# Sink keys as rows of the window products, in units 2 to 7 of a fused attention and MoE kernel

## The chip, the core and the metric

The kernel runs on one core of one Trainium2 chip. Its time is the device time of that core in microseconds (us), the median of the timed runs. TensorE (PE) multiplies matrices: a stationary operand is loaded into the array (the profile lists these loads as PEld), and a moving operand streams past it, one column after the other. ScalarE (ACT), VectorE (DVE) and GpSimd (POOL) do the elementwise work; SyncE (SP) issues most transfers.

## What is computed

Attention over 4 batches of 8 heads, 768 positions, 64 numbers per head; then a two-layer network on the 3072 rows of 512. Heads 0, 2 and 6 are "retrieval" heads with a full causal mask. The other five are "streaming" heads: a query sees the first four keys (the sinks) and the last 64 keys up to itself.

```python
pos = np.arange(S); rel = pos[:, None] - pos[None, :]
causal = rel >= 0
is_sink = pos[None, :] < n_sink                    # 4
in_win = (rel >= 0) & (rel < window)               # 64
stream_keep = causal & (is_sink | in_win)
# retrieval heads: causal; the others: stream_keep
scores = np.where(mask, scale * q @ k.T, -1e9)
a = softmax(scores); attn = a @ v
x = attn.transpose(0, 2, 1, 3).reshape(B * S, H * D)
h = x @ w_in                                       # 512 -> 2048
out = (h * sigmoid(beta * h)) @ w_out              # 2048 -> 512
```

## The kernel before

The work is cut into eight **units** of 384 queries: unit n is batch n // 2 and half u = n % 2. Heads are worked in pairs, `PAIRS = [(0, 2), (1, 3), (4, 5), (6, 7)]`; one head of a pair lies in partitions 0 to 63, the other in 64 to 127. Scores are made transposed: keys on the 128 partitions, queries along the columns.

A planner inside the kernel (`_Plan`) puts all steps of all units in one order before anything is emitted. Each step has a key (`KEYS`, `WEIGHTS`), an engine, a rough cost, and what it needs; the instructions are then emitted in the planned order, and every engine works them off in that order. Where the planner leaves TensorE idle in unit 0's attention, it puts in **filler products** (`fill`), one for each 0.14 us of the gap, whose results are thrown away.

What a pair multiplies in one round (of unit half u), before:

```python
def rounds_of(pi, u):
    if u == 0:
        r = [[("r", 0, 0, 0, 384)], [("r", 1, 0, 128, 256), ("r", 2, 256, 256, 128)]]
    else:
        r = [[("r", j, 0, 0, 384)] for j in range(4)] + [[("r", 4, 0, 128, 256), ("r", 5, 256, 256, 128)]]
    s = []                                   # streaming: one product per 64 keys, up to 128 queries wide
    for c in range(CK * u - u, CK * (u + 1)):
        a = 0 if c == 1 else max(W * c - NQ * u, 0)
        z = min(W * (c + 2) - NQ * u, NQ)
        s.append(("s", c, a, a, z - a))
    kk = [("k", 0, 0, 0, NQ)]                # the sinks of all streaming heads
    if pi == 0: return [(a, a) for a in r]
    if pi == 3:                              # head 6 (retrieval) and head 7 (streaming)
        if u == 0: return [(r[0], s), (r[1], kk)]
        return [(r[0], s), (r[1], r[2]), (r[3], r[4]), (kk, None)]
    return [(s, s)]
```

`r` are retrieval products, `s` streaming ones (64 x 64 tiles of the array, so that four products can run side by side), and `k` the **sink product**: four products of 384 columns on 128 x 32 tiles of the array, with the sink keys in `KS`. Then come `exps` (ACT), `masks` (DVE), and on TensorE the sums of the exponentials and the product with v:

```python
def sums_d(x):                               # units 2 to 7
    for g, heads in enumerate(QUARTERS[x.u]):        # a column group of 32 for each quarter
        # ... one product per head and key block, with `one` as stationary operand
        if not all(RETR[h] for h in heads):
            ops.append((own_k[:, 4 if x.u else g, :], q1, NQ - q1, x.esk[0:96, q1:NQ]))   # the sinks

def pv(x, g):                                # two halves of heads, on 128 x 64 tiles, two side by side
    for t in (2 * g, 2 * g + 1):
        for i, h in enumerate(XT[t]):        # XT = [(1, 0), (2, 3), (4, 5), (6, 7)]
            if RETR[h]: ...                  # all key blocks: 768 columns in u = 0, 1920 in u = 1
            else:
                for m in range(CK):          # CK = 6 windows of 64 queries
                    if m * W == q0:          # q0 = 128 in u = 0, else 0
                        ops[i].append((NQ - q0, dst[:, q0:NQ], v_k[x.b][:, h, :], x.esk[0:96, q0:NQ], True, False))
                    # ... and one product of 64 columns with this window's two bands of v (vb or vs)
```

`v_k` holds the sinks' rows of v. It is made once in each batch by one product of 512 columns (`sink_rows`) and one multiplication on DVE. After `pv`, a unit's output is multiplied by the reciprocals of the sums, which go through DRAM to all partitions (`R`), into `xT`. Then the network: `mm1` (16 steps of four products of 384 columns), tanh on ACT, a multiplication on DVE, `mm2` (48 products of 512 columns), and the store. Steps of the network of earlier units stand between the attention steps of later units.

Of the kernel before, what the change touches and what calls it, by code (L numbers as in the profile page):

```python
# [20 lines left out]
NQ = 384  # L21
W = 64
# [7 lines left out]
ROWS = [16, 1]  # L30
ORDER = [[1, 0, 2, 3, 4, 5, 6, 7], [2, 6, 0, 3, 5, 7, 1, 4]]
# [3 lines left out]
    0: dict(lq=[-867.63, -728.31, -730.63, -861.49], lv=-338.14, C=[-364.52, -1117.07, -416.91, -454.59],  # L35
            T=[-593.39, -494.98, -308.07, -568.52], Q=[-267.24, -212.09, -319.35, -717.68],
            cv=[-309.34, -91.27, -785.19], vs=-175.72, vk=-519.21,
            B=[-492.15, -1098.07, -359.98, -568.46, -655.04, -421.48],
            E=[-761.34, -835.95, -537.15, -373.09, -160.62, -919.99],
            M=[-842.64, -436.28, -451.98, -264.53, -413.76, -592.08], S=-196.54, PV=[-406.98, -335.7], X=-688.47,  # L40
            F=[-47.22, -383.06, -14.57, -520.56], G=[-23.54, 44.75, 33.66, 67.09], H=-87.61, sb=-40.38,
            K=[-295.2, -917.7, -414.78]),
    1: dict(lq=[-424.63, -518.51, -317.21, -542.89], lv=-248.7, C=[-264.93, -110.02, -65.86, 1.78],
            T=[-592.79, -447.04, -134.08, -263.47], Q=[-86.97, -86.77, -472.24, -157.6],
            cv=[-104.39, -123.85, -204.22], vs=-111.06, vk=-227.51,
            B=[-728.8, -332.17, -375.19, -55.98, -37.26, -168.01, -724.86, -812.81, -32.31, -467.05, -96.54],
            E=[-299.76, -955.72, -117.13, -111.14, -506.53, -629.08, -272.67, -374.85, -407.81, -734.1, -557.24],
            M=[-448.13, 142.04, -287.39, -182.14, -214.76, -87.46, -561.74, -248.24, -363, -708.61, -250.48],
            S=-250.99, PV=[-538.57, -518.79], X=-72.99, F=[-62.61, -17.61, 44.38, -2.21],
            G=[58.84, 81.77, 74.93, 65.11], H=-332.45, sb=-201.63),  # L50
    2: dict(lq=[-416.41, -381.4, -375.23, -111.77], lv=-85.57, C=[-1.57, 131.34, 92.08, -0.63],
            T=[-7.79, -106.6, -279.89, -142.17], Q=[-127.57, 11.25, -176.77, -95.2], cv=[215.12, 152.27, -53.69],
            vs=532.03, vk=-98.63, B=[-100.36, -95.37, -260.42], E=[-56.84, -139.67, -194.81],
            M=[-251, -136.27, -105.29], S=-141.35, PV=[-99.98, -73.43], X=58.03, F=[-5.31, 68.88, 61.48, 105.62],
            G=[127.21, 90.09, 155.67, 145.53], R=7.33, K=[-41.03, 176.29, -207.29]),
    3: dict(lq=[-65.67], lv=352.93, C=[276.11, -311.81, -109.25], T=[-65.55, -186.26, 121.75],
            Q=[-27.36, 87.63, -69.21], cv=[303.29, 57.44, 13.83], vs=438.39, vk=191.75,
            B=[-126.86, -132.7, -389.02, -338.32, -42.23, 27.27],
            E=[-174.47, 110.62, -203.94, -257.91, 97.6, -63.29],
            M=[-216.92, -285.73, 28.13, -291.66, -162.48, 133.49], S=5.68, PV=[99.38, 46.54], X=77.71,  # L60
            F=[143.55, 87.99, 21.2, 161.21], G=[211.15, 159.59, 176.38, 124.95], R=-194.75),
    4: dict(lq=[213.64], lv=91.1, C=[-84.25, 214.91, 139.17], T=[-74.73, 137.47, -94.05],
            Q=[-116.26, -18.94, -19.03], cv=[37.21, 191.11, -24.92], vs=216.77, vk=-56.98, B=[63.19, -218.96, 56.7],
            E=[50.2, -22.44, -28.58], M=[-87.34, 62.45, 66.02], S=111.58, PV=[73.02, 72.41], X=-156.66,
            F=[178.96, 228.68, 227.28, 168.93], G=[228.49, 235.2, 212.64, 313.26], R=96.78,
            K=[-98.15, 333.15, -412.12]),
    5: dict(lq=[153.65], lv=283.14, C=[-371.96, 105.69, -99.7], T=[284.77, 136.35, 162.01], Q=[96.7, -6.95, 21.1],
            cv=[343.23, 362.82, 283.36], vs=280.24, vk=315.34, B=[-342.38, -103.18, 138.11, 126.61, -33.02, -1.01],
            E=[151.53, 220.73, 91.89, -241.66, -117.85, 178.48], M=[323.29, 126.63, -48.92, -97.8, -64.06, -284.52],
            S=189.85, PV=[-27.56, 59.94], X=-28.53, F=[246.54, 257.62, 228.44, 218.8],  # L70
            G=[370.19, 298.35, 241.7, 258.69], R=62.41),
    6: dict(lq=[145.75], lv=-48.06, C=[-100.29, 81.71, 55.44], T=[-6.35, -249.03, 190.12], Q=[33.29, 189.15, 130.92],
            cv=[22.17, -39.12, 3.11], vs=-109.11, vk=127.62, B=[-177.6, 246.99, 39.37], E=[252.37, 112.26, 238.38],
            M=[-25.1, 212.24, 357.65], S=68.68, PV=[-104.85, 76.59], X=-95.74, F=[375.04, 260.96, 368.28, 228.57],
            G=[388.65, 85.93, 323.69, 287.02], R=258.28, K=[14.01, -86.57, 0.8]),
    7: dict(lq=[111.55], lv=244.51, C=[-29.06, 38.68, 180.35], T=[-19.82, 321.37, -67.06],
            Q=[-170.86, -20.97, -73.78], cv=[76.79, 160.48, -152.51], vs=345.66, vk=-143.1,
            B=[289.56, 210.32, 223.69, -83.71, -272.2, 113.35], E=[-16, -92.33, -70.04, 333.97, -166.52, 23.53],
            M=[-57.51, -79.37, 15.22, 9.01, 57.77, -43.38], S=105.82, PV=[78.32, 140.51], X=-43.74,
            F=[420.59, 208.13, 325.41, -98.23], G=[328.32, 377.85, 148.63, 178], R=79.15),  # L80
}
WEIGHTS = dict(li=[-240.27, -225.8, -149.08, -105.34], lo=[-231.42, -185.85, -123.74, -8.12],
               ci=[-238.56, -234.45, -195.53, -74.09], co=[-115.86, -8.5, 18.95, 196.17], mask=[-672.86, -114.61],
               esel=-193.69, own=-44.44, sel=-79.94, sink=-196.29, table=-134.62, masks=-67.9, beta=-44.67)
GATES = [30, 47, 50, 64]
# [117 lines left out]
def kernel(  # L203
# [23 lines left out]
    def tpool(name, bufs, space=None):  # L227
# [4 lines left out]
        q2f=5, k2f=5, vf=3, wf=3, c=4, vb=2, vs=2, xT=2, gT=2, t=2, osb=3, R=1, sc=1, rec=1, hl=1, VK=2,  # L232
# [28 lines left out]
    identf = consts.tile([128, 128], F32, name="identf")  # L261
    mask_c = consts.tile([128, 128], BF16, name="mask_c")
    mask_s = [consts.tile([128, NQ], BF16, name=f"mask_s{u}") for u in range(2)]
    esel = consts.tile([128, 8, 4, 8], BF16, name="esel")
    esel_k = consts.tile([96, 4, 8], BF16, name="esel_k")
    beta_h = consts.tile([128, FO], F32, name="beta_h")
    odd = consts.tile([128, W], BF16, name="odd")
    even = consts.tile([128, W], BF16, name="even")
    sel = consts.tile([128, 8, D], BF16, name="sel")
    sel_c = consts.tile([128, 8], F32, name="sel_c")  # L270
    sel_k = consts.tile([128, 4, 2], F32, name="sel_k")
# [4 lines left out]
    own_k = consts.tile([96, 5, 32], BF16, name="own_k")  # L276
    warm = consts.tile([128, 1], F32, name="warm")
    QK = [consts.tile([128, 2, NP, S], BF16, name=f"QK{par}") for par in range(2)]
    KS = [[consts.tile([128, 32], BF16, name=f"KS{par}{pi}") for pi in range(1, NP)] for par in range(2)]
    sink_sel = consts.tile([128, 96], BF16, name="sink_sel")  # L280
    sink_own = consts.tile([96, H], F32, name="sink_own")
# [10 lines left out]
    def const_ident():  # L292
        pool.memset(warm, 0.0)
        pool.memset(identf, 1.0)
        aff(identf, 1, -1, 0, 128)
        aff(identf, -1, 1, 0, 128)
        dve.tensor_copy(out=ident, in_=identf)
# [4 lines left out]
    def const_masks():  # L302
        pool.memset(mask_c, 1.0)
        aff(mask_c, -1, 1, 0, 128)
        pool.memset(odd, 1.0)
        aff(odd, -1, 1, W, W)
        aff(odd, 1, -1, -1, W)
        pool.memset(even, 1.0)
        aff(even[0:W], -1, 1, 0, W)
        aff(even[W:2 * W], 1, -1, -1, W)  # L310
# [4 lines left out]
    def const_own():  # L315

        dve.memset(one, 0.0)
        dve.memset(one[:, 31:32], 1.0)
        dve.memset(own_k, 0.0)
        for u in range(2):  # L320
            for g, heads in enumerate(QUARTERS[u]):
                for i, h in enumerate(heads):
                    if not RETR[h]:
                        pi = [h in p for p in PAIRS].index(True)
                        dve.tensor_copy(out=own_k[:, 4 if u else g, ROWS[u] * i:ROWS[u] * i + 1],
                                        in_=sel_k[0:96, pi - 1, PAIRS[pi].index(h):PAIRS[pi].index(h) + 1])

    def const_zero():
        dve.memset(hl, 0.0)
        for par in range(2):  # L330
            for t in KS[par]:
                dve.memset(t, 0.0)

    def const_mask_s(u):
# [3 lines left out]
        if not u:  # L338
            dve.memset(mask_s[0][W:2 * W, 0:W], 0.0)
            dve.memset(mask_s[0][0:SINK, W:2 * W], 1.0)  # L340
# [98 lines left out]

    held = {}  # L440

    v_k = {}

    def sink_rows(b):

# [680 lines left out]
```

The softmax here doesn't subtract the row's maximum and nothing guards it: scores larger than these inputs give would overflow.

## Time and profile before

| | before |
|---|---|
| median time | 244.4 us |
| span of the profiled execution | 241.3 us |
| PE busy | 230.3 us (95%) |
| ACT busy | 146.4 us (61%) |
| DVE busy | 135.0 us (56%) |
| POOL busy | 79.1 us (33%) |
| transfers | 42.72 MB |

Busy time of PE is time in which at least one product is in the array; a product is counted with its way through the array, so that neighbours overlap. In the timeline the interval from one group's start to the next group's start is therefore the better measure of what a group costs. In the table of time stretches a number after a busy time, such as (x17), counts the instructions that touch the stretch. A tile shape such as 64*64 names the part of the array that a product uses.

### The profile page before, as it was taken

Reading aid. Unit: us, or ns where it says so; the run is one execution under the profiler, and the core shown is the slowest. Engines: PE = TensorE matmul, PEld = TensorE weight load, DVE = VectorE, ACT = ScalarE, POOL = GpSimd, SP = SyncE. Lnnn points to the kernel's source line nnn. Section 1 sums busy time; section 2 is a strip of 40 time slices with the busy share of each in tenths; the row PEclk is TensorE's granted clock in tenths of the full one; section 3 lists DMA queues with packets and bytes.
Section 4 is the critical chain, followed back from the end, with each engine's and each line's share of the span. In section 5 each row is a group of like instructions: output and inputs, shape, how many; then the busy total and the mean of one; then the engine's idle time right before and its main releaser. Section 6 shows DMA issues by size and latency. Waiting matters only on the chain.

```text
span 241.3 us, 5467 instructions
## 1 busy us (share of the span) xinstructions
PE 230.3 (95%) x2124; PEld 128.6 (53%) x2124; DVE 135.0 (56%) x313; ACT 146.4 (61%) x245; POOL 79.1 (33%) x170
## 2 busy tenths in 40 slices
PE   6879997999999999999999999999999999999994
PEld 6656663555444555446544545565465466546553
DVE  5678965788342477623764567576574058406610
ACT  2798762788536398661896278709864138408721
POOL 5233476686754466323745104230000000000000
PEclk9997999999999999999999999999999999999999
DMA  6999999999879997899999969993501620021012
GB/s 193 318 246 211 354 320 284 292 300 209 208 150 236 261 228 178 185 205 251 180 223 217 208 174 233 222 171 113 130 3 48 174 92 0 0 90 43 0 43 87
DMA packets 90570, 42.72 MB, mean 177 GB/s; under 512 B 74592, under 2 KB 83312, under 8 KB 90544
## 3 DMA queue, kind: packets, MB, share of 16 engines
q1 hardware_dynamic: 89424, 41.58, 76.7%
q10 hardware_dynamic: 1120, 0.79, 1.0%
q8 instruction: 16, 0.26, 0.5%
q14 instruction: 10, 0.08, 0.1%
HBM read 31.99 MB, written 6.37 MB: 159 GB/s over the span
## 4 chain that ended last, share of the span: by engine, by line
PE 84%; DMA 6%; ACT 3%; DVE 3%; POOL 2%; SPq 1%; issue 1%; POOLq 0%; ACTq 0%
PE b L103 73%; PE sp L103 11%; DMA wf<-in_moe_w_out_dram 3%; DMA wf<-in_moe_w_in_dram 3%; ACT es L103 2%; DVE QK L103 1%; POOL w_out L103 1%; ACT QK L103 1%; SPq L103 1%; DVE KS L103 0%; DVE b L103 0%; ACT c L103 0%; POOL identf L103 0%; POOL w_in L103 0%; DVE sel L103 0%
## 5 line engine op out<-in xcount | busy, mean ns | idle before, releaser
L103 DVE SCALAR_TENSOR_TENSOR gT<-t,b 128x384 bf16<-128x384 f32 x128 | 69.3, 551 | 51.9 <-ACT t L103 46.3
L103 PE MATMUL b<-xT,w_in 128*128 128x384 bf16 x512 | 89.7, 326 | 1.5 <-POOL w_in L103 1.5
L103 PE MATMUL b<-w_out,gT 128*128 128x512 bf16 (+1 forms) x400 | 90.5, 371 | 0.1
L103 ACT ACTIVATE t<-b,beta_h 128x384 f32<-128x384 f32 x128 | 72.9, 583 | 27.8 <-PE b L103 19.9
L103 PEld LDWEIGHTS <-w_in 128*128 128x128 bf16 x512 | 48.7, 98 | 38.7 <-issue 3.1
L103 PEld LDWEIGHTS <-gT 128*128 128x128 bf16 x400 | 37.3, 98 | 40.1 <-issue 2.9
L103 ACT ACTIVATE es<-sp 128x768 bf16<-128x768 f32 (+1 forms) x68 | 51.1, 799 | 11.9 <-PE sp L103 11.8
L103 ACT ACTIVATE osb<-b 128x512 f32<-128x512 f32 (+1 forms) x21 | 12.1, 578 | 35.4 <-PE b L103 35.3
L103 POOL CAST c<-wf 128x256 bf16<-128x256 f32 x60 | 23.2, 426 | 28.4 <-DMA wf<-in_q_dram 20.5
L103 PE MATMUL sp<-QK 64*64 64x128 bf16 (+5 forms) x420 | 19.6, 245 | 2.2 <-ACT es L103 0.7
L103 PEld LDWEIGHTS <-QK 64*64 64x64 bf16 (+1 forms) x420 | 10.7, 104 | 14.7 <-issue 10.8
L103 POOL CAST vb<-wf 128x512 bf16<-128x512 f32 x18 | 11.8, 686 | 19.0 <-DMA wf<-in_v_dram 16.7
L103 DVE TENSOR_TENSOR es<-es,mask_c 128x256 bf16<-128x256 bf16 (+2 forms) x32 | 10.5, 342 | 13.3 <-ACT es L103 13.2
L103 DVE TENSOR_TENSOR es<-es,mask_s 128x768 bf16<-128x768 bf16 (+1 forms) x24 | 12.9, 541 | 8.8 <-ACT es L103 8.2
L103 PE MATMUL sp<-es,vb 128*64 128x64 bf16 (+3 forms) x228 | 16.2, 246 | 0.0
L103 DVE TENSOR_TENSOR xT<-sp,R 128x768 bf16<-128x768 f32 x12 | 11.3, 956 | 7.2 <-PE sp L103 7.0
L103 PEld LDWEIGHTS <-vb 128*64 128x64 bf16 x228 | 12.1, 113 | 1.3
L103 POOL CAST w_in<-wf 128x512 bf16<-128x512 f32 x16 | 9.2, 617 | 10.2 <-DMA wf<-in_moe_w_in_dram 10.2
L103 POOL COPY vs<-vb 64x1536 bf16<-64x1536 bf16 (+2 forms) x10 | 12.0, 1208 | 0.4
L103 PE MATMUL sp<-es,vs 128*64 128x64 bf16 x120 | 11.3, 199 | 0.0
L103 PEld LDWEIGHTS <-vs 128*64 128x64 bf16 x120 | 9.4, 113 | 1.6 <-issue 1.5
L103 POOL CAST w_out<-wf 128x512 bf16<-128x512 f32 x16 | 9.3, 613 | 2.6 <-DMA wf<-in_moe_w_out_dram 2.5
(83 smaller groups left out, 134.9 us busy)
## 6 DMA issues: line engine op xcount, KB each, us to landing
out_dram<-osb SPq DMA_DIRECT2D x23, 256.0 KB, 2.3
wf<-in_v_dram SPq DMA_DIRECT2D x18, 256.0 KB, 4.7
wf<-in_moe_w_out_dram SPq DMA_DIRECT2D x4, 1024.0 KB, 8.8
wf<-in_q_dram SPq DMA_DIRECT2D x15, 256.0 KB, 4.8
wf<-in_k_dram SPq DMA_DIRECT2D x15, 256.0 KB, 5.1
R<-rd SPq DMA_DIRECT2D x9, 384.0 KB
wf<-in_moe_w_in_dram SPq DMA_DIRECT2D x4, 768.0 KB
q2f<-in_q_dram SPq DMA_DIRECT2D x12, 192.0 KB, 4.7
```

Source lines behind the costliest of these rows:

```text
L103: ins = f(*a, **k)
```

## The change

A query of window m (64 queries) sees, of the band of 64 keys before its own, only keys that are younger than the query's own place in the window. The oldest key of that band is seen by no query of the window, and the next three only by the window's first three queries. In **units 2 to 7** the four rows of these keys now carry the four sinks instead. The stationary operand of the earlier band is a copy of the keys with those rows replaced (`KP`), v is changed in the same places, and the mask lets the sink rows through. The three keys that are lost by this come back as a small **edge product**: the first four queries of the windows (16 columns in u = 0, 24 in u = 1) against the lost keys of all windows. A mask picks the pairs that count. Units 0 and 1 keep the sink product.

The purpose is to have no products of their own for the sinks in scores, sums and `pv`. Streaming scores become two products of 64 columns for each window, where they were one product of up to 128 columns for each band. With this come two shifts of head 6 in u = 1. A copy of its queries and keys in the other half of the partitions (`QD`) lets its score products run side by side with each other. The last 128 of its queries (`moved`) run in the other half of the columns in `pv`. All keys of the planner are new, and with them the order of steps in all units, the weights' transfers and the fillers too.

```diff
+NE = [16, 24]
 KEYS = {                     # ... every number is new; WEIGHTS and GATES too
-GATES = [30, 47, 50, 64]
+GATES = [28, 43, 53, 79]
 ...
+    def sink_v(x):                                   # DVE, once in each of the units 2 to 7
+        dve.tensor_copy(out=x.vs[W:W + SINK, j0:, 1:H], in_=vb[0:SINK, 0:1, 1:H].to_broadcast([SINK, n, H - 1, D]))
+        dve.tensor_copy(out=vb[0:SINK, t0:t0 + n, 1:H:2], in_=vb[0:SINK, 0:1, 1:H:2].to_broadcast([SINK, n, H // 2, D]))
+        dve.tensor_copy(out=vb[0:SINK, t0:t0 + n, 4], in_=vb[0:SINK, 0:1, 4].to_broadcast([SINK, n, D]))
+    def load_edge(b, u):                             # three transfers of 8 x 8 x 64, six in each batch 1 to 3
+        ...
+    def kp_copy(x, pi, eng):                         # POOL or DVE, pairs 1 to 3 of units 2 to 7
+        cast(eng, dst[:, :, SINK:], kt[:, c0:c0 + n * W].rearrange("p (m n) -> p m n", n=W)[:, :, SINK:])
+        cast(eng, dst[:, :, 0:SINK], kt[:, 0:SINK].unsqueeze(1).to_broadcast([128, n, SINK]))
+        cast(eng, KP[pi - 1][:, NQ:].rearrange("p (a k) -> p a k", a=8), _view(kt, t0, [[1, 8], [st, 8]]))
+    def qd_copy(x):
+        dve.tensor_copy(out=x.QD[D:128], in_=x.QK[0:D, :, 3, NQ:S])
 ...
-    def rounds_of(pi, u):
+    def rounds_of(pi, n):
+        k = "d" if pi == 3 and n >= 2 else "r"       # "d": from QD
+        s = [("s", c, W * (c - CK * u), W * (c - CK * u), W) for c in range(CK * u, CK * (u + 1))]
+        kk = [("k", 0, 0, 0, NQ)] if n < 2 else None
-            return [(r[0], s), (r[1], r[2]), (r[3], r[4]), (kk, None)]
+            return [(r[0], s), (r[1], r[3]), (r[2], r[4])]          # n >= 2
 ...  scores
+                elif kind == "s":
+                    for c in (kb - 1, kb):           # two products of 64 columns for a window
+                        ops[i].append((ps[r:r + W, i, col:col + n], l, rhs))
+                for j in ([0, 1] if pi == 3 else [i]):               # the edge product
+                    for r in (0, W):
+                        ops[j].append((ps[r:r + W, j, NQ:NQ + ne], l, rhs))
 ...  sums_d
-            if not all(RETR[h] for h in heads):
-                ops.append((own_k[:, 4 if x.u else g, :], q1, NQ - q1, x.esk[0:96, q1:NQ]))
+                    ops += [(one[...], 0, NQ, x.work[h]), (one[...], None, NE[x.u], x.edge[h])]
 ...  pv
+                    cut = 256 if moved(x, h) else NQ                 # head 6 in u = 1
-                            ops[i].append((NQ - q0, dst[:, q0:NQ], v_k[x.b][:, h, :], x.esk[0:96, q0:NQ], True, False))
+                        if x.n < 2 and m * W == q0:
+                            todo.append((NQ - q0, dst[:, q0:NQ], VE[x.b][0:96, h - 1, :], x.esk[0:96, q0:NQ]))
+                    todo.append((NE[x.u], dst[...][:, CK - nb:, 0:SINK], VE[x.b][:, h - 1, :], x.edge[h]))
 ...  norm, u = 1, second half: four multiplications for one
-        dve.tensor_mul(x.xT[:, 2 * g:2 * g + 2, :], o[:, :, 0:NQ], x.R[:, 2 * g:2 * g + 2, :])
+        dve.tensor_mul(x.xT[:, 2, :], o[:, 0, 0:NQ], x.R[:, 2, :])
+        dve.tensor_mul(x.xT[:, 3, 0:256], o[:, 1, 0:256], x.R[:, 3, 0:256])
+        dve.tensor_mul(x.xT[D:128, 3, 256:NQ], o[D:128, 1, 256:NQ], x.R[D:128, 3, 256:NQ])
+        dve.tensor_mul(x.xT[0:D, 3, 256:NQ], o[D:128, 1, NQ:512], x.RX[D:128, :])
 ...
-        if not u:                                    # sink_rows and sink_copy in every batch
+        if n == 0:                                   # only in batch 0
```

## The prediction

> **What bounds the kernel now.** I read four views in this order: the page's busy times and slices, TensorE's waits, the timeline of TensorE around unit 2's attention, and the table of time stretches.
>
> ```profile
> PE 230.3 (95%) x2124; PEld 128.6 (53%) x2124; DVE 135.0 (56%) x313; ACT 146.4 (61%) x245; POOL 79.1 (33%) x170
> ...
> PE   6879997999999999999999999999999999999994
> PEld 6656663555444555446544545565465466546553
> DVE  5678965788342477623764567576574058406610
> ```
>
> PE is busy 95% of the span. In the slices (6.03 us each) it is under nine tenths in the first three, the seventh and the last only. DVE is near full in some of the first ten slices, and later never for long.
>
> ```profile
> PE b L103 <- DVE xT L103: 2.2, 1, 2.2
> PE b L103 <- POOL w_in L103: 1.5, 2, 1.0
> PE sp L103 <- ACT es L103: 0.9, 3, 0.5
> PE sp L103 <- ACT QK L103: 0.6, 2, 0.4
> ```
>
> PE's waits are few and short: the start (2.2, `xT` is the blank tile of the first fillers), 1.5 us for w_in, and some for exponentials and copies of units 0 and 1. The same question asked from 60 us to the end gives no wait. So from 57 us on the time is the sum of PE's work. A column taken off PE there comes off the end, and nothing another engine saves does.
>
> ```profile
> 59.78 0.52 PE L103 MATMUL sp<-QK 64*64 64x384 bf16 x12
> 60.22 0.35 PE L103 MATMUL sp<-QK,KS 128*32 128x384 bf16 x4
> 60.50 0.42 PE L103 MATMUL b<-vb,sink_sel 128*96 128x512 bf16 x1
> 60.75 2.75 PE L103 MATMUL b<-w_out,gT 128*128 128x512 bf16 x12
> ```
>
> Start to start, unit 2's sink product costs 0.28 us and its `sink_rows` 0.25.
>
> ```profile
> 63.44:64.16 0.72, 0.72 (x20) 1.00 1.24 349
> 80.38:81.76 1.38, 1.38 (x46) 1.00 1.27 283
> 86.32:87.10 0.78, 0.78 (x12) 1.00 1.18 267
> 88.50:88.78 0.28, 0.28 (x6) 1.00 0.96 219
> 107.87:110.33 2.46, 2.46 (x56) 1.00 1.24 231
> ```
>
> These stretches are, in order, unit 2's sums, unit 2's `pv`, head 6's later rounds in unit 3, unit 3's sink product, and unit 3's `pv`. All are PE-bound at full clock (1.00).
>
> **What the Trainium skill says.**
> - "TensorE: Matmul & The Clock Gate", section Back-to-back issue gap: a warm product costs N/2.4 + 2.5 ns, but about 25 ns at least. The trace agrees for wide ones: 16 products of 384 columns from 33.97 to 36.58 us are 163 ns each (formula 162.5). No row of before shows the floor for 16 or 24 columns.
> - "TensorEngine Tiling (Array Packing)", section Key Properties: different tiles load and multiply in parallel, and a change of tiling mode drains the array. The trace agrees: 24 score products, mostly of 128 columns, took 0.49 us (57.47 to 57.96), 20 ns each, where one alone would need 56. Nine w_out products between two attention groups took 2.04 us (73.81 to 75.85), 0.10 more than 9 x 216 ns.
> - "SBUF — State Buffer", section SBUF: two separate sides: DVE and GpSimd share a port pair that one locks for a whole instruction. The new `KP` copies on either engine can thus delay the other; no row of before measures by how much.
>
> **The change part by part, PE first.** Columns are of the slower of the tiles that run side by side; 2.4 columns are 1 ns.
>
> *Units with u = 0 (2, 4, 6).* The sink product goes: -0.28. `sink_rows` goes: -0.24 (0.25 here; 0.22 in unit 4, 77.59 to 77.81). Sums: the fullest column group held 768 (retrieval) + 384 + 256 (sinks) = 1408 columns and now holds 1152 and an edge of 16: -232 columns, -0.10. `pv`: 1408 columns in each half become 1168, so -480, -0.20. Streaming scores: per tile and pair, 3 products of 128 (384 columns, 168 ns by the formula) become 6 of 64 (175 ns) and an edge (25 ns). That is +0.032 per round, +0.065 for pairs 1 and 2 and +0.03 for pair 3. Sum: -0.28 - 0.24 - 0.10 - 0.20 + 0.095 = **-0.72**.
>
> *Units with u = 1 (3, 5, 7).* Sink product: -0.28. Head 6's rounds from the second on: 1536 columns one behind the other (0.78 us) become 768 with `QD` in the other row half: -768 columns, -0.32. Sums: the fullest group had 5 x 384 + 384 = 2304, now 5 x 384 + 5 x 24 = 2040: -0.11. `pv`: its first half goes from 768 + 1920 = 2688 columns to 408 + 1920 = 2328. Its second goes from 768 + 1920 = 2688 to 1584 (head 6 keeps 1152 beside head 4's 408; the 768 moved ones lie beside heads 5 and 7 with 408 each). That is -1464 columns, -0.61; a few more products take back 0.03. Scores +0.095. Sum: -0.28 - 0.32 - 0.11 - 0.58 + 0.095 = **-1.20**.
>
> Three of each: 3 x (-0.72 - 1.20) = **-5.8 us**. In the order of instructions, TensorE changes between kinds of work 119 times before and 100 after. The removed sink products and `sink_rows` account for 14 of these and are counted. The other five at 0.10 us would be -0.5, but some lie in the start, so I take -0.2.
>
> *Beside PE.* DVE and POOL get the `KP` copies (for one unit, nine small instructions). A POOL copy runs at about 1 ns an element (1462 ns for 1536), so 360 + 24 + 64 elements for each of three pairs are about 1.3 us plus starts, an estimate of 2.3 us. On DVE, `sink_v` copies 1536 elements a partition in u = 0 and 2304 in u = 1; 1536 took 550 ns in `vs`, so about 0.6 to 1.0 us. `norm` in u = 1 goes from 0.96 to perhaps 1.45 us. In all DVE and POOL have some 3 to 4 us more in 20; in stretches of 20 us after 60 us DVE is busy 7 to 14 us and POOL 12 at most. ACT loses the sink half of its exponentials (about 0.4 us a unit) and gains 16 or 24 columns on others: even. The edge transfers are 18 of 16 KB, next to 42.72 MB. All that lies beside PE if it comes in time.
>
> *The start.* Units 0 and 1 have the same arithmetic as before, in a new order. Fillers rise from 63 to 73. Ten more at the planner's 0.14 us say that it expects 1.4 us more idle PE in unit 0's attention, most before the first w_in product (eleven fillers there while unit 1's q and k are awaited). Against this, w_in now comes before most of w_out in the transfers, so the two waits for w_in (1.5 us) should go. Before unit 2's first score both orders have the same network work done: 24 `mm1` steps and 15 `mm2` products, at 54.3 us in before. Up to there the transfers run without pause (DMA share about 1.0 from 10 to 60 us) and carry the same bytes, so I expect that moment within 1.5 us of 54.3. I set the start to 0, with that spread.
>
> *The sum.* -5.8 - 0.2 + 0 (start), and +0.5 for new waits of an order with copies never timed before: -5.5. 244.4 - 5.5 = **238.9 us**.
>
> **The rivals.**
> 1. *Narrow products are bound by issue, not by columns.* Unit 2's pairs 1 and 2 go from 24 products to 56. If each pair of load and product cost the 15 to 20 ns seen now, the burst would cost 0.85 to 1.1 us, not 0.49; per pair of units some 1 us would be lost, 3 to 4 us in all: about 242. For it: the skill's floor of 25 ns. Against it: with 128 columns over four tiles, 320 ns of the 490 are columns and most of the rest is drain, and in `pv` two products of 64 columns side by side start every 30 ns, which is 64/2.4 + 2.5. I give it one in eight.
> 2. *The new copies become the wait.* `KP` has one buffer: a unit's copies wait for the scores of the unit before and precede its own. If they come late, PE, which works in order, stands still before the 56-product burst, six times. For it: the shared port, and POOL instructions behind casts that wait for transfers (20.5 us for q alone). Against it: between two units' scores lie 10 us and more of network work. One us per two units would make it 240 to 242.
> 3. *The start gets longer*, since unit 1's inputs now stand behind two loads of w_in: +2 to +3 us, 241 to 242. For it: the fillers. Against it: the shorter wait for w_in and equal bytes.
> 4. *The start gets shorter*: the early w_in keeps PE full from the first `mm1` on: 236 to 237.
>
> **Range and chances.** The PE sum in the saturated part is arithmetic with measured rates, good to about 0.8 us. The start is good to 1.5, and stalls can only add. That gives 236.0 to 242.2 for eight in ten. 2% faster is 239.5 us, close to my middle, so faster by over 2% gets 0.58 and within 2% 0.38. Slower by over 2% (over 249) needs stalls of 10 us, for which nothing speaks: 0.04.
>
> **What would show it right or wrong.** In the profile after: unit 2's burst of 56 products near 0.55 us (over 0.8 is rival 1); `pv` of 1.2 us in u = 0 and 1.9 in u = 1; head 6's later rounds 0.45; no 128*32 sink product after unit 1; PE busy about 5 us less, and no waits over 0.3 us after 60 us (waits on `KP`, `vb` or `VE` copies are rival 2); unit 2's first score near 54 us (rivals 3 and 4). The prediction fails if PE has waits of more than 2 us in sum after 60 us, or if the start moves by more than 2 us.

## The result, and the profile after

The changed kernel takes **247.0 us** (median of 4 runs, 246.1 to 247.5) where the kernel before takes 244.4: a ratio of 1.011, with a 95% interval of 1.007 to 1.016. Predicted were 238.9 us and a range of 236.0 to 242.2. The change makes the kernel slower by one per cent, and the prediction missed by 8 us, outside its range. Ratios here and below compare kernels on one chip and leave out runs more than 1.5% above the fastest of their kernel, while medians are of all runs; where the two say different things (e4, e13, e15), the text gives both.

The page of the changed kernel, busy times and slices (6.1 us each):

```profile
PE 225.5 (92%) x2349; PEld 128.5 (52%) x2374; DVE 150.9 (61%) x351; ACT 147.4 (60%) x246; POOL 83.3 (34%) x194
...
PE   7696898879899999799899979999999999999994
...
DVE  2779579983547675735597447869675448637300
...
PEclk9869799999999999999999999999999999999999
DMA  6999898999859989999999892999615207011022
```

And one row of the page before that the prediction did not show:

```profile
DMA  6999999999879997899999969993501620021012
```

Compare three things. PE, at nine tenths from the eighth slice on before, now has gaps up to the 24th (147 us). The granted clock (`PEclk`) dips to 0.6 in the third slice. And the row of the kernel before shows what the prediction passed over: the 16 DMA engines are close to full for 27 slices, up to 163 us. TensorE was not the only thing that was full. (The page after lists 2349 of 2374 products, so its 225.5 us of PE are low; a second run of the changed kernel, called *the second run* below, has all of them, and 229.1 us.)

TensorE's waits in the changed kernel, longest groups (total us, times, longest us):

```profile
PE b L113 <- DVE gT L113: 3.9, 4, 1.6
...
PE sp L113 <- ACT es L113: 1.9, 4, 0.7
PE sp L113 <- ACT QK L113: 1.8, 1, 1.8
PE sp L113 <- DMA QK<-c: 1.7, 1, 1.7
```

After 60 us, where the kernel before had none, there are waits for gT (2.3 us) and for a transfer (1.7 us), and some for copies (`issue` is time in which TensorE waited for nothing that the profile shows, here where products are missing).

The table of stretches for the second run: unit 2's burst of 56 score products, its sums, head 6's later rounds in unit 3, unit 2's `pv`, unit 3's `pv` (PE, PEld, DVE, ACT, POOL busy, clock, DMA share, GB/s):

```profile
66.74:67.33 0.59, 0.59 (x58) 0.57 (x57) 0.00 (x0) 0.48 (x1) 0.00 (x0) 1.00 0.53 108
70.24:70.86 0.62, 0.62 (x20) 0.41 (x20) 0.55 (x1) 0.04 (x1) 0.00 (x0) 1.00 0.47 85
85.92:86.37 0.45, 0.45 (x11) 0.26 (x10) 0.13 (x1) 0.04 (x1) 0.45 (x1) 1.00 1.09 249
87.77:88.99 1.22, 1.22 (x46) 1.14 (x46) 1.12 (x1) 0.07 (x1) 1.22 (x2) 1.00 1.25 304
110.70:112.62 1.92, 1.92 (x59) 1.89 (x59) 1.21 (x2) 0.09 (x1) 0.00 (x0) 1.00 1.39 202
```

Each is near what the prediction said: 0.59 us (0.55), 0.62 (0.72 - 0.10), 0.45 (0.45), 1.22 (1.2), 1.92 (1.9). So the work on TensorE did get shorter, and the time got longer. Adding up start-to-start times in the two traces gives the account (us):

| | before | second run of the changed kernel | difference | predicted |
|---|---|---|---|---|
| start, to unit 2's first score | 54.3 | 59.2 | +4.9 | 0 |
| score products, units 2 to 7 | 13.7 | 12.4, of it 0.9 waits | -2.2 without them | -2.1 |
| `sink_rows` | 0.7 | - | -0.7 | -0.7 |
| sums | 5.6 | 5.0 | -0.6 | -0.6 |
| `pv` | 11.5 | 9.4 | -2.1 | -2.3 |
| waits after the first score, all else | | | +5.0 | +0.3 |
| span | 241.3 | 245.7 | +4.4 | -5.5 |

The last wait row is what is left of the span. 4.2 us of it show directly: the network stretches after 54 us, with the same 813 products, take 156.2 us instead of 152.0. The other 0.9 us are the two waits among the scores. The -5.6 us on TensorE are there, and two losses of 5 us each stand against them. From the first score to the end both traces of the changed kernel take 186.4 us, where the kernel before takes 187.0: almost nothing of the saving is left there. The start's +4.9 is less certain than it looks, since it is the difference of two traces, and the start moves from run to run in both kernels, as the part on the prediction shows.

**Where the waits come from.** The timeline of the second run around 95 us, SyncE's issues (`SPq`), then DVE and PE:

```profile
84.41 5.79 SPq L113 DMA_DIRECT2D wf<-in_k_dram  x2
90.25 1.17 SPq L113 DMA_DIRECT2D vf<-in_v_dram  x3
...
91.99 2.58 SPq L113 DMA_DIRECT2D wf<-in_v_dram  x3
94.67 1.75 SPq L113 DMA_DIRECT2D rec<-sc  x2
...
98.04 0.35 DVE L113 RECIPROCAL rec<-rec 96x32 f32<-96x32 f32 x1 [1.43 <-DMA rec<-sc]
98.31 0.95 DVE L113 SCALAR_TENSOR_TENSOR gT<-t,b 128x384 bf16<-128x384 f32 x2
...
98.85 1.46 PE L113 MATMUL b<-xT,w_in 128*128 128x384 bf16 x8 [0.85 <-DVE gT L113]
```

Read it from the bottom. TensorE waits for a bank that DVE's swish (gT) frees; DVE works in order and stands 1.43 us at the reciprocals; these wait for the row sums' transfer `rec<-sc`, which SyncE issued only at 94.67, although TensorE had the sums done at 90.1 and ScalarE had copied them out by 90.6: it stood behind block loads of k, edge loads and v. The issue of two k loads alone takes 5.79 us, of which one takes 4.81; what held it, the profile does not show. The wait is labelled gT, and its source is the transfer side. Around 141 us the same happens with the transposes:

```profile
131.52 4.47 SPq L113 DMA_DIRECT2D vf<-in_v_dram  x6
136.91 4.00 SPq L113 DMA_TRANSPOSE QK<-c  x3
...
142.90 0.50 PE L113 MATMUL sp<-QK 64*128 64x384 bf16 x6 [1.65 <-DMA QK<-c]
```

A row of this view runs from the first start to the last end. Six edge loads of 16 KB fill 4.47 us here, but their issues take only 0.27 to 0.38 us each, 2.0 us in all. In the rest, and before the transposes that follow, SyncE waits for earlier transfers to land (its waits from 131.4 to 136.9 us):

```profile
SPq L113 <- DMA R<-rd: 2.3, 2, 1.4
SPq L113 <- DMA wf<-in_k_dram: 0.9, 1, 0.9
```

TensorE then waits 1.65 us for the transposes.

### The profile page after: what moved, and what is told of

It is laid out like the page before. It is cut to its first block, busy times and chain, and to the rows that moved or that the text cites. A ratio compares the mean times of both kernels' runs of the same rounds, so it can differ in the third digit from the quotient of the medians.

```text
span 245.4 us, 6044 instructions
## 1 busy us (share of the span) xinstructions
PE 225.5 (92%) x2349; PEld 128.5 (52%) x2374; DVE 150.9 (61%) x351; ACT 147.4 (60%) x246; POOL 83.3 (34%) x194
## 4 chain that ended last, share of the span: by engine, by line
PE 69%; DMA 11%; DVE 9%; ACT 4%; SPq 2%; issue 2%; ACTq 1%; POOL 0%; DVEq 0%; POOLq 0%
PE b L113 59%; PE sp L113 10%; DMA QK<-c 3%; DMA R<-rd 3%; SPq L113 2%; DMA rec<-sc 2%; DMA k2f<-in_k_dram 2%; DVE gT L113 2%; ACT es L113 2%; DMA vf<-in_v_dram 2%; DVE mask_s L113 2%; ACT t L113 1%; DVE vs L113 1%; DVE KP L113 1%; ACTq L113 1%
## 5 line engine op out<-in xcount | busy, mean ns | idle before, releaser
L113 PE MATMUL b<-w_out,gT 128*128 128x512 bf16 (+1 forms) x375 | 87.1, 370 | 4.2 <-issue 1.9
L113 ACT ACTIVATE es<-sp 128x768 bf16<-128x768 f32 (+2 forms) x64 | 48.2, 806 | 15.3 <-PE sp L113 15.1
L113 POOL CAST c<-wf 128x256 bf16<-128x256 f32 x60 | 23.7, 438 | 22.9 <-DMA wf<-in_k_dram 12.4
L113 PE MATMUL sp<-QK 64*64 64x64 bf16 (+7 forms) x402 | 19.8, 245 | 4.8 <-ACT QK L113 1.8
L113 DVE TENSOR_TENSOR es<-es,mask_c 128x256 bf16<-128x256 bf16 (+2 forms) x32 | 12.5, 394 | 16.3 <-ACT es L113 16.1
L113 DVE TENSOR_TENSOR es<-es,mask_s 128x800 bf16<-128x800 bf16 (+5 forms) x24 | 12.8, 535 | 5.6 <-ACT es L113 5.3
L113 POOL COPY KP<-QK 128x64 bf16<-128x64 bf16 (+5 forms) x32 | 9.0, 322 | 18.5 <-DVE gT L113 12.3
L113 DVE TENSOR_TENSOR xT<-sp,R 128x768 bf16<-128x768 f32 (+3 forms) x18 | 11.6, 686 | 4.8 <-PE sp L113 3.4
L113 PE MATMUL sp<-es,vb 128*64 128x64 bf16 (+3 forms) x243 | 14.3, 241 | 0.0
L113 ACT COPY QK<-b 128x384 bf16<-128x384 bf16 (+1 forms) x17 | 8.6, 539 | 4.9 <-PE b L113 3.1
L113 DVE COPY vs<-vb 64x1536 bf16<-64x1536 bf16 (+4 forms) x21 | 10.9, 529 | 0.3
```

The lines of the kernel that those rows point to most:

```text
L113: ins = f(*a, **k)
```

## The experiments

Two theories at first. **A**: the saving is eaten by single waits, each of which can be taken away by its own cause. **B**: up to about 155 us the transfers (SyncE's issues and the DMA engines) are a second bound just beneath TensorE, so that a wait taken away in one place comes back in another. Later a third joined for the start: the clock.

**e1: masks not built again.** In the change DVE rebuilds the two masks in the start (1.2 to 2.1 us each in e5 and the second run).

```diff
     def const_mask_new(u):
+        return
```

> The changed kernel without the building of the new masks (their six to seven small DVE operations in two places; the masks keep the old rows and zero tails, so sinks and edges of units 2 to 7 are masked wrongly). Theory A, the saving on TensorE is real and is spent in single waits, each of which comes straight off the end when removed: the wait of 1.5 us before the first w_out product at 55 us goes, and some 1.7 us of the waits around the hl products at 42 to 45 us; 247.0 - 3.2 = 243.8 us, and unit 2's first score moves from 59.0 to about 56. Theory B, the transfers and their issue bound the units from 60 us on: unit 2's first score comes earlier all the same, but the time falls by less than 1 us, to 246 or more, and the waits after 60 us grow by what the start gained.

245.57 us, ratio 1.010 (1.007 to 1.014). The wait near 53 us goes and unit 2's first score comes at 57.8 instead of 59, but the waits near 97, 120 and 140 stay, at 1.9, 0.4 and 1.7 us. The start of this trace is 1.2 to 1.4 us shorter; from there to the end it takes 186.8 us, the changed kernel 186.4. Between the two expectations.

**e2: part of the masks on GpSimd.**

```diff
-        dve.memset(e, 0.0) ... tensor_add(e[:, :, 0], ...)      # the edge columns
+        pool. ...                                               # earlier, in unit 0
```

> The changed kernel with the new masks built on GpSimd: the edge columns during unit 0, when GpSimd is idle, and only two small memsets per mask at the old places; complete computation. Theory A: nearly all of what leaving the masks out brings, about 244.2 us. Theory B: 246 or more.

246.64 us, ratio 1.015 (1.010 to 1.020): no gain. In the trace (of a run of 248.8 us) the first score came at 60.6, later than without the edit, and the waits near 99, 122 and 142 us are still there, with 1.2, 0.8 and 1.7 us. A's 244.2 is missed.

**e3: the row sums' transfer issued by ScalarE.**

```diff
-            sp.dma_start(out=x.rec[...], in_=x.sc[...])
+            act.dma_start(out=x.rec[...], in_=x.sc[...])
```

> The changed kernel with the transfer of the sums (rec<-sc) issued from ScalarE's queue instead of SyncE's, where it stands behind loads; same work. Theory A: the reciprocals on DVE no longer hold up the gT multiplications behind them at 98 and 121 us, so the waits of 1.7 and 0.9 us of TensorE go: 247.0 - 2.4 = 244.6 us. Theory B: the waits move to the transposed loads of q and k (QK<-c) and the time stays within 1 us of 247.

249.45 us, ratio 1.026 (1.021 to 1.031). Of the waits after 60 us those for gT are gone, and there is this instead, where the changed kernel had 1.7:

```profile
PE sp L113 <- DMA QK<-c: 3.6, 2, 1.9
```

The wait moved from the sums to the transposes, as B has it; A expected 244.6. SyncE issued the transposes for unit 4 at 97.06 us, in the second run at 97.01, so TensorE only came to them earlier and then waited 1.93 us. The new loss lies behind that wait. The same twelve products of `w_out` in the second run, then in e3:

```profile
103.50 2.76 PE L113 MATMUL b<-w_out,gT 128*128 128x512 bf16 x12
103.55 4.45 PE L113 MATMUL b<-w_out,gT 128*128 128x512 bf16 x12
```

The granted clock from 103.5 to 107.5 us is 0.57 in e3. That is 1.7 us, and from the first score to the end e3 takes 188.2 us, 1.8 more than the changed kernel. In this trace the clock, not a longer wait, made it slower.

**e4: without the 18 edge loads** (the edge keys' v rows are zero).

```diff
-        for a in range(3):
-            sp.dma_start(out=held["e", b][...], in_=...)
+        if not u:
+            dve.memset(held["e", b][0:48], 0.0)
```

> The changed kernel without the 18 edge loads of v (their rows are zero, so the three lost keys are missing in the product with v; the rest is computed). Theory A: the wait of 1.8 us for QK<-c at 141 us goes, the others stay: 245.2 us. Theory B: SyncE's queue is freed of 18 issues of about 0.65 us each, and as it sets the pace all waits after 60 us shrink: 243 us or less.

244.48 us, ratio 1.001 (0.997 to 1.004); that leaves out six of 13 runs, and the medians of all (244.48 beside 242.97) give 1.006. 0.3 MB out of 43, in 18 small transfers, and some 2 us come back: from the first score to the end the trace takes 184.3 us instead of 186.4, and no wait of over 0.6 us is left after 60 us. More than A expected, and less than B. (The 18 issues take 0.36 us each in the second run, not the 0.65 of the expectation.)

**The changed kernel again**, unaltered, beside the next three.

> The changed kernel once more, unaltered, beside the experiments on one chip. Every theory: a ratio near 1.011 to the kernel before; unit 2's first score near 59 us; the granted clock at 0.5 to 0.7 for some microseconds after each of the two idle stretches of TensorE in the start (6.8 to 8.8 us and 20 to 23 us); waits of 1.7 and 1.8 us near 97 and 141 us.

247.12 us, ratio 1.016 (1.012 to 1.020).

**e5: more fillers in the start.** The prediction had not looked at what idle TensorE does to the clock. The table of stretches for the second run of the changed kernel, then for e5 (columns as above):

```profile
10.00:15.00 5.00, 4.13 (x54) 2.84 (x52) 3.84 (x12) 4.43 (x10) 2.72 (x8) 0.60 1.28 259
15.00:20.00 5.00, 5.00 (x65) 2.86 (x66) 4.08 (x13) 4.35 (x8) 0.89 (x3) 0.50 1.05 328
```

```profile
10.00:15.00 5.00, 4.09 (x75) 2.95 (x73) 4.57 (x13) 4.72 (x10) 2.99 (x9) 1.00 1.27 257
15.00:20.00 5.00, 4.29 (x86) 2.74 (x86) 4.57 (x13) 4.73 (x9) 0.80 (x2) 1.00 1.03 319
```

```diff
-            fill(ps[:, 0, 0:128])                        # ahead of unit 0's first score
+            fill(ps[:, 0, 0:128], 30 if pi == 1 else 0)  # and 60 more in four other places
```

> The changed kernel with 90 more filler products in five places of the start where TensorE stood idle; nothing else moves. Clock theory (idle TensorE brings the granted clock to half for 4 to 6 us afterwards, and the work done at half clock makes the start longer): the clock stays at 1.00 in 10 to 17 and in 22 to 27 us, unit 2's first score comes 2 to 3 us earlier (56 to 57 us instead of 59), the time falls by as much, to about a ratio of 1.00, and the runs spread less. Order theory (the start waits for loads, exponentials and copies in the new order, and the clock is only a symptom): the clock is full, the first score stays within 1 us of 59 us, and the ratio stays at 1.008 to 1.015.

The clock is full, and unit 2's first score comes at 57.0 instead of 59.2. That part of the clock theory holds in direction: with TensorE kept busy there is no half clock, and the start is shorter. Its size is less sure. The changed kernel's unaltered start gave 58.1 to 59.2 in five traces (itself twice, e3, e4, e10), so 1.1 to 2.2 us, and among these five the clock does not order the starts: granted over the first 60 us were 0.89 in e3 and 0.94 in e10, and both have the first score at 58.1. In the second run TensorE stands idle for 2.2 us from 6.7 us on, and the clock is at 0.60, then 0.50, in the next ten microseconds. (The Trainium skill, "TensorE: Matmul & The Clock Gate", Part 1, puts the fall to half clock after an idle window of about 3.4 us, and the return after as much sustained work; here a gap of 2.2 us, in a stretch busy for 2.3 of 5 us, was enough.) But the time fell only to 246.39 us, ratio 1.013 (1.007 to 1.018), where the clock theory had about 1.00: from the first score to the end e5 takes 187.4 us, the changed kernel 186.4. So 1.0 us is given back behind the start, where near 97, 119, 137 and 141 us there are now waits of 1.4, 1.1, 1.0 (in two parts) and 1.6 us. This is what B says of a faster start.

**e6: fillers, no edge loads, no new masks** (e1, e4 and e5 together).

> The changed kernel with the fillers, without the 18 edge loads and without the second building of the masks (output incomplete). If the extra time is the sum of the clock, the mask waits and the edge loads: about -2.5 -1.5 -2 from the changed kernel's 247, some 241 us, a ratio of 0.985 to 0.99, so slightly under the kernel before. If the start is bound by the order: 243.5 to 245, a ratio of 1.00 to 1.005.

241.93 us, ratio 0.996 (0.994 to 0.999). First score at 55.8, and 184.0 us from there to the end. Better than the order alone allows, and short of the 0.985 to 0.990 of the sum of the three.

**e7: the start's old priorities.** All parts of the change, with the keys of the kernel before for units 0 and 1 and the weights.

```diff
-    0: dict(lq=[-821.83, ...   1: dict(lq=[-506.07, ...
+    0: (keys of the kernel before)   1: (keys of the kernel before)
```

> All parts of the change, but units 0 and 1, the constants and the weights take the priorities of the kernel before (the order after unit 2's first score also comes out different, with no tuning behind it). Order theory: unit 2's first score comes near 54 to 56 us and the start's 4.7 us come back; the later part may gain waits of its own, so the total is 241 to 246. Theory that the new start is forced by the change's parts themselves: first score again at 58 us or later, total 247 or more.

275.44 us, ratio 1.134. A miss as an experiment: the later order comes apart, with waits of 10 and 7 us. All that can be read is that the first score came at 58.5, so the old priorities alone did not bring the old start back.

**e8 and e9: TensorE work taken out of the kernel before.** If TensorE alone bounds the kernel before, as the prediction said, a microsecond less of its work is a microsecond off the end, wherever it lies. e8 cuts most sum products of units 2 to 4, e9 those of units 5 to 7 (one product a column group is kept).

```diff
             assert ops[0][1:3] == (0, NQ)
+            if x.n in (2, 3, 4):                          # e9: (5, 6, 7)
+                ops = [(mask_c[:, 96:128], 0, NQ, ops[0][3])]
```

> The kernel before, with most of the sum products of units 2, 3 and 4 left out (one product a column group is kept; output incomplete): 1.66 us of TensorE columns less, all before 140 us, the order unchanged. If TensorE alone bounds that part, the time falls by about 1.7 us (ratio 0.993). If the transfers, whose share is about 1.0 up to 155 us, bound it as much as TensorE does, TensorE only waits longer: a fall of 0.5 us or less (ratio 0.998 or more) and new waits of TensorE before 160 us.

> The same cut in units 5, 6 and 7: 2.03 us of TensorE columns less, most of it after 155 us, where the transfers' share falls to 0.46 and below. Both theories: a fall of 1.7 to 2.1 us (ratio 0.991 to 0.993).

e8: 243.56 us beside 242.98, ratio 1.003 (1.000 to 1.007). 1.66 us of TensorE work before 140 us are worth **nothing**. e9: 242.32 us, ratio 0.995 (0.993 to 0.998), so about 1.1 us of 2.03 come off, less than either theory expected. From the first score to the end the traces agree: 187.0 us before, 186.9 in e8 and 186.0 in e9. The trace of e9 shows which part was lost. Unit 5's part, 0.80 us, lies at 141 us, before the transfers ebb. The timeline of e9:

```profile
140.81 0.35 PE L103 MATMUL b<-es,mask_c 128*32 128x384 bf16 x4
141.91 0.50 PE L103 MATMUL sp<-QK 64*128 64x384 bf16 x6 [0.75 <-DVE KS L103]
```

The sums are 0.8 us shorter, and TensorE at once waits 0.75 us for a copy of DVE, which has worked without a pause since 138.2 us. Here it is DVE, not a transfer, that is only just in time. What is left, 1.23 us in units 6 and 7, agrees with the 1.1 us that came off. In the trace of e8 (a run of 246.7 us, above its median), DVE and then TensorE:

```profile
100.59 0.35 DVE L103 RECIPROCAL rec<-rec 96x32 f32<-96x32 f32 x1 [1.98 <-DMA rec<-sc]
101.40 0.81 PE L103 MATMUL b<-w_out,gT 128*128 128x512 bf16 x2 [1.40 <-DVE gT L103]
```

It is the chain that the change made visible, without the change. Under TensorE there was next to no slack.

**e10 and e11: transfers taken out.** The output stores of units 0 to 4 (15 of 256 KB) are left out of the changed kernel (e10) and of the kernel before (e11).

```diff
     def out_store(x, ns):
+        if x.n in (0, 1, 2, 3, 4):
+            x.ob.pop(ns)
+            return
```

> The changed kernel without the output stores of units 0 to 4 (15 transfers of 256 KB left out; output incomplete). If transfers bound it between 55 and 155 us: the waits near 97, 120 and 141 us go, and the time falls by 3 us or more (ratio to the kernel before 1.003 or less). If its waits are each a matter of one order: a fall of 1 us or less (ratio 1.011 or more).

> The kernel before without the same 15 stores (output incomplete). TensorE has no waits after 60 us there, so under either theory the time stays within 0.7 us (ratio 0.997 to 1.000); a fall of 2 us or more would mean that transfers, not TensorE, bounded the kernel before.

e10: 243.27 us, ratio 0.999 (0.996 to 1.002), beside the 1.011 and 1.016 of the changed kernel: 3 to 4 us off, although no product and no order on TensorE changed. TensorE's waits after 60 us, but for `issue`:

```profile
...
PE sp L113 <- DMA QK<-c: 0.4, 1, 0.4
PE b L113 <- DVE QK L113: 0.4, 1, 0.4
PE sp L113 <- DVE KP L113: 0.3, 1, 0.3
PE b L113 <- DVE gT L113: 0.2, 1, 0.2
```

Every wait of over half a microsecond is gone, those labelled gT too. The DMA share of 80 to 140 us is hardly lower than in the changed kernel (0.99, 1.16, 1.07 in steps of 20 us, against 0.98, 1.09, 1.07). It falls from 0.81 to 0.45 between 160 and 180 us: what was behind moved up. e11: 242.32 us, ratio 0.997 (0.995 to 1.000), 0.6 us. So in the kernel before TensorE was still first and the transfers right behind; in the changed kernel the transfers are first.

**e12: everything blamed so far left out**: the edits of e6 and of e10 together.

> The changed kernel with the fillers and with everything left out that the runs so far blame: no 18 edge loads, masks not built again, no output stores of units 0 to 4 (output incomplete). The kernel before without the same stores stood at a ratio of 0.997. If start, masks and transfers account for the whole loss, the 4.8 us of TensorE work now show against that: a ratio of 0.975 to 0.985. If something else eats them: 0.99 or more.

239.64 us, ratio 0.985 (0.981 to 0.989); six runs within 0.9 us. From the first score to the end it takes 181.8 us. The fair partner is e11, the kernel before without the same stores, with 186.3 us there. The difference is **4.5 us**: most of the 5.6 us of TensorE work, now that little else is in the way. As whole times the gain is 0.985 against 0.997, or 3 us, because the first score still comes at 55.7 where e11 has 53.3.

**e13: fillers, and the masks moved.** Nothing is left out from here on. The masks of u = 1 are built after unit 2's sums; those of u = 0 in two parts between early DVE instructions.

```diff
+        for g, g2 in [(("const", "new", 1), [("sum_s", 2)]), (("const", "new", 0), [("g", 0, 3), ("xT", 0, 3)])]:
+            ...                                          # put the step behind the steps named
```

> Complete output: the fillers, and the masks of u = 1 built after unit 2's sums and those of u = 0 in two parts between early instructions of VectorE, instead of ahead of the reciprocals and of the last network steps. Start theory: unit 2's first score near 56 us instead of 57. If transfers bound what follows, most of that is given back near 95, 118 and 140 us: a ratio of 1.007 to 1.012. If not: 1.004 or less.

246.39 us, from 242.1 to 249.1; ratio 1.003 (0.998 to 1.009), which rests on four of 15 runs, while the medians of all (246.39 beside 243.19) give 1.013. So the two expectations cannot be told apart. The first score comes at 56.4 and the wait near 53 is gone, and near 95, 117, 136 and 140 us there are waits of 0.7, 1.1, 0.5 and 1.7 us. The runs, all at a clock of 0.99 or more, lie 7 us apart, against 0.9 us in the six of e12. That speaks against the clock as what spreads the times; that it is the transfers is not shown.

**e14 and e15: the edge loads issued by GpSimd**, and in e15 the row sums' transfer by ScalarE as in e3.

```diff
-            sp.dma_start(out=held["e", b][...], in_=...)
+            pool.dma_start(out=held["e", b][...], in_=...)
-            sp.dma_start(out=x.rec[...], in_=x.sc[...])      # e15 only
+            act.dma_start(out=x.rec[...], in_=x.sc[...])
```

> The run before with the 18 edge loads issued by GpSimd instead of SyncE; the bytes stay. If what the edge loads cost is SyncE's 4 us of issue ahead of the transposes and sums: as without edge loads, a ratio of 0.998 to 1.003. If it is the transfers themselves: little changes, 1.005 to 1.012. New risk: GpSimd's casts wait behind its issues.

> The run before with the row sums' transfer to rec issued by ScalarE too. Alone this moved the wait from the sums to the transposes (1.026). With the edge loads off SyncE, the transposes no longer stand behind them: order theory 0.995 to 1.000; transfer theory 1.000 to 1.01, with a wait elsewhere.

e14: 243.98 us, ratio 1.003 (1.000 to 1.006). e15: 242.86 us, ratio 0.993 (0.990 to 0.996) on ten of 22 runs; the medians of all (242.86 beside 243.19) give 0.999. Against e14 it is 1.1 us faster by the medians. So the edit that made e3 slower does no harm here and probably gains: the transposes for unit 4 are issued at 92.38 us, with no edge loads ahead of them, and TensorE's waits for them are gone (0.7 us in e14, 3.6 in e3). e14 against e13 stays open: the medians are 2.4 us apart, the ratios the same. In e15 one wait for gT is left, 1.4 us at 91 us. The timeline of GpSimd and DVE there:

```profile
88.33 2.99 POOL L113 COPY vs<-vb 64x1536 bf16<-64x1536 bf16 x2
...
91.36 0.62 DVE L113 COPY vs<-vb 4x1344 bf16<-4x1344 bf16 x1 [2.13 <-POOL vs L113]
```

DVE stands 2.13 us at `sink_v`, one of the change's new copies, since GpSimd makes `vs` late, and the swish waits behind it. GpSimd itself had issued three edge loads from 85.98 us on, for 1.67 us: the risk that the expectation of e14 named.

**e16 and e17: unit 3's `sink_v` behind twelve of unit 2's swish instructions** instead of ahead of them (the first expectation says four). e16 is e15 with it, e17 is e14 with it.

```diff
-        for g, g2 in [(("const", "new", 1), ...), (("const", "new", 0), ...)]:
+        for g, g2 in [(("const", "new", 1), ...), (("const", "new", 0), ...), (("vk", 3), [("g", 2, 11)])]:
```

> e15 with unit 3's sink_v (VectorE copies that wait for GpSimd's vs) moved behind four more instructions of VectorE, so that unit 2's swish no longer waits behind it at 91 us; complete output. If that 1.6 us wait is on the path: a ratio about 0.005 lower than e15's, 0.985 to 0.990. If transfers set the pace at this point too: no change, 0.991 to 0.997, and the wait appears later.

> The same with the row sums' transfer to rec back on SyncE (so e14 with sink_v later); complete output. If rec's place on SyncE still matters without the edge loads: 0.003 to 0.01 above e16. If not: the same as e16 within the intervals.

e16: **241.60 us beside 243.10 of the kernel before, ratio 0.993** (0.991 to 0.996), with the whole of the change in it. e17: 243.29 us, ratio 1.002 (0.999 to 1.004). In e16 the wait at 91 us is gone:

```profile
PE sp L113 <- DVE xT L113: 0.9, 2, 0.5
PE b L113 <- DVE gT L113: 0.6, 1, 0.6
```

The ratio did not fall below e15's. By the medians of all runs it did, from 0.999 to 0.994, which is the 0.005 expected of a wait on the path. So that question stays open. What the pair settles is the issue: the same bytes, with the row sums' transfer off SyncE's queue, are worth 0.8% (intervals apart). So it is at least in part SyncE's order, not only the amount of data. How much of the transfer bound is the 16 DMA engines and how much the one queue, these runs don't separate. Nor is 0.993 the worth of the change alone: the fillers and the transfer on ScalarE were not tried in the kernel before.

## Why the prediction was wrong

Its arithmetic on TensorE was right: -5.6 us measured, -5.8 predicted, each term within 0.25 us. (In one sum 1408 less 1152 and 16 columns is 240, not 232; the 0.10 us stays.) Rival 1 (narrow products bound by issue) is refuted: 56 products in 0.59 us. Both signs that it had named for its failure came: waits of 4.6 and 3.8 us in sum after 60 us in the two traces, and a start later by more than 2 us.

**The step that failed is the first one**: "So from 57 us on the time is the sum of PE's work. A column taken off PE there comes off the end, and nothing another engine saves does." It followed from a true reading, no waits of TensorE after 60 us. But no waits only says that the others are in time, not by how much. e8 shows the sentence wrong in the kernel before itself: 1.66 us of columns out, nothing gained. The evidence stood in the prediction's own table, one column further: the stretches are quoted with a clock of 1.00 and, beside it, DMA shares of 1.24, 1.27, 1.18, 0.96 and 1.24. The text used the first and not the second. (A high share alone proves no bound, as e10 shows; taking transfers or products out does.) "What 'DMA-bound' means" in the Trainium skill ("Perfetto Trace Analysis", section Optimizing DMA Performance) names both forms of it, the DMA engines and the issuing engine's sequencer; here both agree: from 55 to 150 us the main queue's packets take 106% of the 16 engines' time in the kernel before (they overlap in the records) and 99% in the changed one, and SyncE's transfer instructions take 85 of the 95 us before and 76 in the second run.

**"Next to 42.72 MB" mis-sized the edge transfers.** By bytes they are 0.7%. By SyncE's time they are 6.5 us in the second run, and six at a bad place take 4.5 us with the waits between them; leaving all 18 out was worth some 2 us (e4).

**"I set the start to 0" failed, by 4.9 us between the two traces.** Rival 3 named the direction (2 to 3 us), but gave a reason that no run tested. Two parts had not been in the sum at all: the masks on DVE ahead of what TensorE needs stood in the diff without a cost, and the fillers were read as a forecast of idle time, not as what keeps the clock up. With fillers, and the masks left out or moved, the first score comes at 55.4 to 56.5 us in seven traces (e6, e12 to e17); with the start as the change has it, at 58.1 to 59.2 in five. So the two together are some 2.7 us. What each is worth rests on single traces (e5: 1.1 to 2.2; e1: 0.3 to 1.4). How much is left for the new order stays open, because the kernel before, with nothing changed in its start, had its first score at 53.3, 54.3, 55.8 and 58.0 us in four traces (e11, itself, e9, e8).

**"+0.5 for new waits" was 5.0.** Rival 2 was right in kind and small at first: waits on `KP` of 0.2 to 0.4 us, and 1.4 us behind `sink_v` when others were gone (e15).

The range was too narrow for the same reason. It came from the spread of TensorE's terms, and "stalls can only add" was given half a microsecond in a kernel whose transfers were about as full as TensorE.

## What to carry to other kernels

An engine at 95% without waits is a bound, but perhaps not the only one. Before work taken off it is booked as gain, look at the DMA share of the same stretches and at the issuing queue, and cut some of its work in the kernel before to see what comes off the end. Count a small transfer by the time that it, and what it waits for, holds the queue in front of what is urgent, and work in a start by the idle time that it leaves on TensorE as well. See how far a stretch moves between runs of one kernel before a difference of two traces is given a cause.

## What was not expected of the hardware

- In the two traces of the changed kernel TensorE was idle for 1.8 and 2.2 us near 7 us, and busy for 1.7 of the 3.5 us and 1.6 of the 3.4 us before the clock fell. The clock was then 0.50 for 7 and 10 us. 90 fillers removed it. In e3 one wait of 1.93 us at 103 us was followed by half clock and cost another 1.7 us.
- Of two block loads of 256 KB, one held SyncE for 4.81 us; 17 of the second run's 18 edge loads of 16 KB took it 0.27 to 0.48 us each (one took 0.99), and three of them took GpSimd 1.67 us to issue (e14, e15).
- A DVE addition on only 128 x 6 or 128 x 4 numbers (the new masks) took 0.17 us where GpSimd stood idle meanwhile (e13 to e17) and 0.41 to 0.53 us where GpSimd was casting meanwhile (e3, e5). The prediction had named such a delay (rival 2) without a size.
